# A tuned Fourier-and-MLP kernel: one forward product and a second inverse table for batch 0, angles by integer shifts, filter copies by GpSimd in one row

## The chip, the cores and the metric

One core of one Trainium2 chip. The metric is the time of one execution on the device in microseconds (us), the median of several. "Dense stage" below is the MLP part, which fills most of the time; "prologue" is what batch 0 needs before it.

## The reference, cut to what matters

```python
# x: (8, 3008, 256), filt_r, filt_i: (1505, 256), w_in: (256, 2048), w_out: (2048, 256)
X = np.fft.rfft(x, axis=1)
y = np.fft.irfft(X * (filt_r + 1j * filt_i)[None], n=3008, axis=1)   # per batch
h = y.reshape(-1, 256) @ w_in
out = (0.5 * h * (1 + erf(h / sqrt(2)))) @ w_out                      # (24064, 256)
```

The transform is done as matmuls over 3008 = 47 x 64. For batches 1 to 7 its four stages (s1 to s4, with two trips through HBM, "R") are strewn between the matmuls of the dense stage. Batch 0 has nothing to hide behind: its stages c1, c1t, c2, c3, c3t and c4 stay on the chip and are the prologue.

## The kernel before

Cuts are marked "...".

```python
def load_filters(self, k0, k):          # 4 DMAs from GpSimd into partitions 0..63 of F
    ...
def dup_filters(self, eng, k0, k):      # copies to partitions 64..127, two k at a time
    for k in range(k0, k0 + k, 2):
        o, i = (self.F[r:r + 64, :, k:k + 2, :].rearrange(...) for r in (64, 0))
        eng.tensor_copy(out=o, in_=i)

def c2(self, p):                        # forward product of batch 0, times the filter
    ps = self.bank("ps_c2", "w")        # two banks: plain and turned by a quarter
    for t, o in ((0, 1), (1, 0)):
        for i in range(2):
            nc.tensor.matmul(ps[:, t, ...], lhsT=self.T2[:, k, o:o + 2]..., rhs=...)
    nc.vector.tensor_tensor(out=w, in0=ps, in1=f, op=ALU.mult)          # 128 x 1024

def s1(self, b, c):                     # first stage of batch b >= 1, in slots of the dense stage
    a = self.pa.tile([128, 2, 4, 256], BF16, tag="a", name="a_sb")      # pa has 3 buffers
    ...                                 # matmuls to PSUM, VectorE evicts to a, SyncE writes a to R

# the order on GpSimd's queue
m.load_x(0, 1, 4); ...
for k, n in ((0, 4), (4, 4), (8, 8), (16, 8)):
    m.load_filters(k, n)
m.dup_filters(nc.gpsimd, 4, 4)
m.load_w_in()
m.dup_filters(nc.gpsimd, 8, 8)
...
m.dup_filters(nc.gpsimd, 16, 8)
...                                     # T1p, table_1_tiles
m.load_x(1); m.load_w_out(0); m.load_w_out(8)
```

Batch 1's s1 runs at slots 1, 5, 9 and 13 of the dense stage (a slot is one pair of matmuls into ps_h); the second matmul of the MLP, which reads w_out, starts at slot 16.

## Time and profile before

| | before |
|---|---|
| median | 773.57 us (four runs, 773.46 to 776.69) |
| first dense matmul starts | 40.55 us |
| TensorE busy from there on | without a hole |
| R writes of batch 1, issue to landing | 2.0 to 4.1 us, median 2.6 |

The prediction shows the page and the chain. TensorE in the timeline of the kernel before (start, length, engine, line, operation, names, shape, count; in brackets the idle time ahead and what ended it):

```profile
49.62 1.47 PE L461 MATMUL ps_h<-y_sb,w_in_sb 128*128 128x512 bf16 x6
50.92 0.60 PE L488 MATMUL ps_o<-w_out_sb,g_sb 128*128 128x256 bf16 x4
```

VectorE's timeline of the same kernel:

```profile
46.74 4.87 DVE L247 CAST a_sb<-ps_s 128x512 bf16<-128x512 f32 x8 [0.29 <-PE ps_s L272]
```

The eight evictions into a_sb of the third and fourth s1 stand in one piece: no buffer is missing.

### The profile page before, as it was taken

How to read it: one execution, taken by the hardware profiler on the slowest of the kernel's cores; microseconds unless marked ns; L12 is line 12 of the kernel's file. 1: busy time of each engine (PE TensorE's matmuls, PEld its weight loads, DVE VectorE, ACT ScalarE, POOL GpSimd, SP SyncE). 2: the span in 40 equal slices, each digit the busy share in tenths (PEclk: the TensorE clock that was granted, in tenths of full speed). 3: DMA queues.
4: the chain of work that ended last, by engine and by line, in shares of the span. 5: the costliest groups of instructions: out<-in, count | busy, mean ns of one | idle time of the engine just before them, and what ended most of it. 6: DMA issues, size and time to landing. Idle time of an engine off the chain costs nothing.

```text
span 772.2 us, 15059 instructions
## 1 busy us (share of the span) xinstructions
PE 763.2 (99%) x6066; PEld 528.7 (68%) x6066; DVE 397.3 (51%) x722; ACT 567.4 (73%) x981; POOL 64.9 (8%) x160
## 2 busy tenths in 40 slices
PE   8999999999999999999999999999999999999998
PEld 4847675676776766677777776666776776766666
DVE  7866755464555645457463664637646366411011
ACT  6879955897568975699656996579865798666663
POOL 7801100020000200011000110001100000000000
PEclk9999999999999999999999999999999999999999
DMA  8894745466253661636516464255553422410111
GB/s 138 145 180 124 150 123 129 128 124 151 57 139 107 138 159 41 192 78 122 143 53 181 85 133 123 79 154 95 124 137 81 139 83 69 123 42 28 42 42 55
DMA packets 87398, 85.66 MB, mean 111 GB/s; under 512 B 6752, under 2 KB 77536, under 8 KB 87328
## 3 DMA queue, kind: packets, MB, share of 16 engines
q1 hardware_dynamic: 78816, 68.70, 31.0%
q0 software_dynamic: 8512, 16.00, 14.9%
q8 instruction: 47, 0.77, 0.4%
q14 instruction: 23, 0.19, 0.1%
HBM read 54.00 MB, written 46.66 MB: 130 GB/s over the span
## 4 chain that ended last, share of the span: by engine, by line
PE 94%; DMA 3%; POOL 2%; issue 0%; DVE 0%; POOLq 0%
PE ps_o L488 43%; PE ps_h L461 42%; PE ps_s L345 2%; PE ps_s L320 2%; PE ps_s L295 2%; PE ps_s L272 2%; DMA x_sb<-in_x_dram 2%; POOL F L96 1%; POOL x_sb L82 1%; DMA F<-in_filt_i_dram 1%; POOL F L91 0%; PE ps_e L478 0%; POOL T1s L258 0%; DVE ost L501 0%; POOL T1p L580 0%
## 5 line engine op out<-in xcount | busy, mean ns | idle before, releaser
L464 ACT ACTIVATE g_sb<-ps_h 128x512 bf16<-128x512 f32 x752 | 438.0, 597 | 182.8 <-PE ps_h L461 172.1
L488 PE MATMUL ps_o<-w_out_sb,g_sb 128*128 128x256 bf16 x2992 | 447.5, 273 | 0.0
L461 PE MATMUL ps_h<-y_sb,w_in_sb 128*128 128x512 bf16 (+3 forms) x1600 | 445.8, 366 | 0.7 <-DMA x_sb<-in_x_dram 0.7
L488 PEld LDWEIGHTS <-g_sb 128*128 128x128 bf16 x2992 | 283.9, 98 | 134.3 <-issue 9.9
L461 PEld LDWEIGHTS <-w_in_sb 128*128 128x128 bf16 x1600 | 154.7, 98 | 23.7 <-issue 1.1
L494 DVE COPY ost<-ps_o 128x512 f32<-128x512 f32 x93 | 63.8, 686 | 143.5 <-PE ps_o L488 143.4
L303 DVE TENSOR_TENSOR p<-ps_s,F 128x512 bf16<-128x512 f32 x84 | 58.1, 691 | 105.9 <-ACT p L302 89.5
L249 DVE TENSOR_SCALAR y_sb<-ps_s 128x376 bf16<-128x376 f32 x112 | 60.9, 548 | 80.5 <-PE ps_s L345 80.5
L247 DVE CAST a_sb<-ps_s 128x512 bf16<-128x512 f32 x112 | 69.3, 682 | 27.7 <-PE ps_s L272 27.7
L247 DVE CAST v_sb<-ps_s 128x512 bf16<-128x512 f32 x84 | 57.4, 684 | 2.9 <-PE ps_s L320 2.6
L301 ACT ACTIVATE p<-ps_s 64x512 bf16<-64x512 f32 x84 | 49.9, 594 | 2.1
L302 ACT CAST p<-ps_s 64x512 bf16<-64x512 f32 x84 | 48.5, 577 | 1.0
L345 PEld LDWEIGHTS <-d_sb 96*128 96x128 bf16 x448 | 30.8, 97 | 25.3 <-DMA d_sb<-R 0.2
L101 POOL COPY gate<-p 1x1 bf16<-1x1 bf16 x48 | 8.5, 178 | 470.3 <-DVE p L305 470.3
L305 DVE TENSOR_TENSOR p<-p 128x512 bf16<-128x512 bf16 x84 | 35.7, 425 | 2.9
L345 PE MATMUL ps_s<-T,d_sb 96*128 96x94 bf16 x448 | 36.3, 204 | 0.0
L304 DVE TENSOR_TENSOR p<-p,F 128x512 bf16<-128x512 bf16 x84 | 34.8, 415 | 0.0
L82 POOL DMA_DIRECT2D x_sb<-in_x_dram x64 | 32.7, 512 | 13.0 <-issue 12.5
L320 PE MATMUL ps_s<-p,T 128*128 128x256 bf16 x168 | 32.1, 273 | 0.0
L295 PE MATMUL ps_s<-b_sb,T 128*128 128x256 bf16 x168 | 32.1, 273 | 0.0
L320 PEld LDWEIGHTS <-T 128*128 128x128 bf16 x168 | 16.4, 98 | 20.1 <-DVE p L305 0.5
L295 PEld LDWEIGHTS <-T 128*128 128x128 bf16 x168 | 16.4, 98 | 13.4
(103 smaller groups left out, 189.1 us busy)
## 6 DMA issues: line engine op xcount, KB each, us to landing
out_dram<-ost SPq DMA_DIRECT2D x93, 256.0 KB, 2.3
x_sb<-in_x_dram POOLq DMA_DIRECT2D x64, 188.0 KB, 3.8
R<-a_sb SPq DMA_DIRECT2D x112, 96.0 KB, 2.1
b_sb<-R SPq DMA_DIRECT2D x28, 384.0 KB, 4.3
R<-v_sb SPq DMA_DIRECT2D x42, 256.0 KB, 3.5
d_sb<-R SPq DMA_DIRECT2D x56, 192.0 KB, 4.7
w_in_sb<-in_moe_w_in_dram POOLq DMA_DIRECT2D x2, 512.0 KB, 7.8
w_out_sb<-in_moe_w_out_dram POOLq DMA_DIRECT2D x2, 512.0 KB, 11.3
```

The source lines that it names most:

```text
L247: self.nc.vector.tensor_copy(out=out, in_=in_)
L249: self.nc.vector.tensor_scalar(out=out, in0=in_, scalar1=scale, scalar2=None, op0=ALU.mult)
L295: nc.tensor.matmul(ps[:, 256 * i:256 * i + 256], lhsT=self.T2[:, k, 1:3].rearrange("p a b -> p (a b)"), rhs=self.st[b, "b", k // 6][:, k % ...
L301: nc.scalar.activation(out=p2[0:64], in_=ps[64:128], func=AF.Copy, scale=-1.0)
L302: nc.scalar.copy(out=p2[64:128], in_=ps[0:64])
L303: nc.vector.tensor_tensor(out=p1, in0=ps, in1=f(0), op=ALU.mult)
L320: nc.tensor.matmul(ps[:, 256 * i:256 * i + 256], lhsT=self.T3[:, k].rearrange("p a b -> p (a b)"), rhs=w[:, 256 * i:256 * i + 256], start= ...
L345: nc.tensor.matmul(ps[:, 94 * i:94 * i + 94], lhsT=d[:, (grp % 2) * 4 + i, 128 * half:128 * half + 128], rhs=t4, start=True, stop=True)
L461: nc.tensor.matmul(ps[:, o:o + n], lhsT=self.w_in_sb[:, dc, jc * 128:jc * 128 + 128], rhs=self.ring[:, dc, off:off + n], start=(dc == 0), ...
L464: nc.scalar.activation(out=self.st["g", t][:, jc, :], in_=ps, func=AF.Gelu)
L488: nc.tensor.matmul(ps[:, tile_i % 2, :], lhsT=g[:, jc, tile_i * 128:tile_i * 128 + 128], rhs=self.w_out_sb[:, jc, :], start=(jc == 0), sto ...
L494: nc.vector.tensor_copy(out=ost, in_=ps)
```

## The change

Intent: batch 0 gets one product in c2 instead of two. The quarter turn moves to the inverse side: T3i is T3 with its halves exchanged and signed, so c3 multiplies the second filter part by T3i. The angles of table 2 are made so large (64 turns are added) that a shift of the float's bits left by 15 leaves the fraction of a turn as an integer, in place of a rounding and a subtraction. GpSimd gets small operations, some of which VectorE and ScalarE had, copies all but the first filters in one row, and issues w_in only after it. Gelu's table load moves behind c3. Fillers on TensorE replace part of the work taken away.

```diff
-        self.T2 = c.tile([128, K1, 3, NB], BF16, name="T2")
+        self.T2 = c.tile([128, K1, 2, NB], BF16, name="T2")
@@ table_2_angle @@
-        v.tensor_scalar(out=r, in0=w, scalar1=RND, scalar2=-RND, ...)
-        v.tensor_tensor(out=w, in0=w, in1=r, op=ALU.subtract)
+        ts(out=self.gen[:, 1, k].bitcast(I32), in0=w[:, k].bitcast(I32), scalar1=15, scalar2=None,
+           op0=ALU.logical_shift_left)
@@ c2 @@
-        for t, o in ((0, 1), (1, 0)):
-            for i in range(2): ...            # four matmuls into two banks
+        for i in range(2): ...                # two matmuls into one bank
-            nc.vector.tensor_tensor(out=w, in0=ps, ...)
+            nc.vector.tensor_tensor(out=w, in0=ps.unsqueeze(1).to_broadcast([128, 2, 512]), ...)
@@ c3 @@
+                        t3 = (self.T3i if t else self.T3)[:, 2 * (p + i) + k]
@@ order of the prologue @@
-    m.p = m.iota(g, "p", ...)
-    m.load_x(0, 0, 1, (0,))
+    m.load_x(0, 0, 8)
+    m.p = m.iota(g, "p", ...)
...
+    m.load_filters(0, 4)
+    m.turn_signs(g)                           # 5 small operations on GpSimd
+    m.weights_4(g)                            # 4, before on VectorE
+    nc.gpsimd.tensor_copy(out=m.T1q, ...)     # before on ScalarE
+    nc.gpsimd.memset(m.vt[:, :, 96, :], 0.0)  # before behind the loads
+    for k, n in ((4, 4), (8, 8), (16, 8)):
+        m.load_filters(k, n)
+    m.dup_filters(nc.gpsimd, 4, 20)
...
+    m.table_4(m.T4c, m.T1q, m.wtc, "n", False)   # VectorE evicts, after c3; before ScalarE, earlier
...
+    m.load_w_in()                             # before: after the second filter copy
     m.load_x(1)
```

## The prediction

> **What bounds the kernel now.** I read the page first, then the chain of waits in order of time for the first 80 us, then the timeline of each engine up to 62 us, last the DMA landings in the stretch where the chain turns into DMA.
>
> The page says that TensorE bounds the kernel, at full granted clock:
>
> ```profile
> span 772.2 us, 15059 instructions
> PE 763.2 (99%) x6066; PEld 528.7 (68%) x6066; DVE 397.3 (51%) x722; ACT 567.4 (73%) x981; POOL 64.9 (8%) x160
> ...
> PE 94%; DMA 3%; POOL 2%; issue 0%; DVE 0%; POOLq 0%
> ```
>
> That is no use for this change: its diff touches only the prologue (batch 0 through the Fourier stages). The chain of waits shows what the prologue hangs on, from 5.88 us to the first matmul of the dense stage:
>
> ```profile
> 5.88 7.07 DMA x_sb<-in_x_dram
> ...
> 15.36 5.87 DMA F<-in_filt_i_dram
> ...
> 21.36 1.88 POOL F L96 x2
> ...
> 24.30 4.99 POOL F L96 x5
> ...
> 30.24 2.98 POOL x_sb L82 x6
> 33.22 7.24 DMA x_sb<-in_x_dram
> 40.46 0.09 issue
> 40.55 0.59 PE ps_h L461 x2
> ```
>
> Columns: start, length, what. The reader is to see a row of deliveries: x of batch 0, then the filters, then GpSimd's copies of the filters to the upper 64 partitions. The last link (x of batch 1, landing 40.46) I do not believe: the first matmul of the dense stage reads only the ring and w_in. VectorE's timeline gives another candidate that ends at the same instant, 39.23 + 1.17 = 40.40:
>
> ```profile
> 16.72 4.82 DVE L388 TENSOR_TENSOR p<-ps_c,F 128x1024 bf16<-128x1024 f32 x4
> 22.43 6.88 DVE L388 TENSOR_TENSOR p<-ps_c,F 128x1024 bf16<-128x1024 f32 x6 [0.88 <-POOL F L96]
> 29.61 1.23 DVE L388 TENSOR_TENSOR p<-ps_c,F 128x1024 bf16<-128x1024 f32 x1 [0.30 <-POOL F L96]
> 30.75 1.27 DVE L392 TENSOR_TENSOR p<-ps_c,F 128x512 bf16<-128x512 f32 x2
> ...
> 33.69 5.56 DVE L247 COPY d_sb<-ps_c3t 96x1024 bf16<-96x1024 bf16 x8 [0.75 <-PE ps_c3t L424]
> 39.23 1.17 DVE L249 TENSOR_SCALAR y_sb<-ps_c 128x376 bf16<-128x376 f32 x2
> ```
>
> So the real path is: filters k = 8 to 15 land at 21.23; one GpSimd copy; from 22.43 VectorE multiplies eight steps almost without a hole to 32.02; a fixed tail of 8.4 us (the last of c3, the transposes, the last inverse stage) to 40.4; then TensorE without a hole to the end. VectorE waited 0.88 us before the fifth multiplication, so everything that ended earlier than 22.43 has 0.9 us to spare. Whatever moves 40.55 moves the end one for one; nothing else does, unless TensorE gets a hole later.
>
> **What the Trainium skill says.** "VectorE: DVE Perf Modes", section "Why PSUM operands drop a tier": an fp32 operand in PSUM holds the multiplication at one element a cycle. Its formula for the fp32 two-tensor add, (N+151)/0.96, gives 1224 ns for 1024 elements; the trace has 1217. So reading one bank twice instead of two banks once should not make it shorter. "ScalarE: Activation LUTs", section "What ACT_TABLE_LOAD costs": 1283 ns a load; the trace has 1283 ns. "DMA: Bandwidth & Descriptors", section "Issuing engines are not separate DMA queues": transfers of all queues run on the same 16 engines and interleave. The trace agrees: at 44 to 46 us the software queue has 118% and the hardware queue 20% of the engines' time. "TensorE: Matmul & The Clock Gate", section "What's actually happening": an idle TensorE falls to half clock. The fillers before and after are there for this; in the trace the fillers and matmuls from 7.3 us run at the fast rate (16 small matmuls in 0.84 us against 1.44 for the first 16), and I expect no change.
>
> **The change part by part.**
>
> *One product instead of two in c2.* 48 matmuls of 256 columns become 24. In the timeline four take 0.60 us, about 0.43 without the pipeline's tail, so 24 x 0.108 = 2.6 us leave TensorE. Two to three fillers of 512 columns a step of the loop come in, 0.21 us each: 0.43 + 0.21 = 0.64 us for 0.43 saved. TensorE per two multiplications: 0.43 (c2) + 0.44 (8 transposes) + 0.89 (16 matmuls of 128 columns) + 0.64 = 2.4 us while transposes last, 2.0 after; VectorE needs 2 x 1.15 = 2.3. I followed four steps from 22 us with two banks for c2: each product is ready 0.1 to 0.6 us before VectorE asks. On the path: 0.
>
> *Second inverse table, T3i.* Two of three parts are turned by ScalarE (four evictions of 256 elements, about 0.4 us each), one by VectorE (two small ones). Against that go two extra evictions of the swap (0.5 us each) and one copy of 0.35. ScalarE comes out level, and lies in the slack. On the path: 0.
>
> *Angles by a shift.* For each half 0.56 (rounding) and 0.96 (subtraction) go, a shift of about 0.6 comes: VectorE is free about 1.9 us earlier, ahead of the first evictions. But c1 waits for x (the last of it lands at 12.96), and after c1 there is the 0.9 us of slack. On the path: 0.
>
> *Gelu's table load* moves from 14.51 to the end of c3. There ScalarE idles 2.29 us, against 1.28 + 0.20: hidden. It makes c1t(1) about 1.4 us earlier, within slack.
>
> *Two x loads ahead of all iotas.* In the row before the first issue starts at 1.33 and the second at 2.11, after two iotas. After, I put the first at about 0.9 and the third 0.7 to 0.9 earlier. From 4 us to 28 the DMA engines are full, so the whole row comes earlier by about 0.45: x done 12.5 instead of 12.96, filters k = 8 to 15 at 20.8 instead of 21.23. GpSimd's new small operations (about 11, some 1.7 us) stand in the 2.8 us in which it waited for x landings between filter issues, so they cost nothing.
>
> *Copies in one row.* The w_in issues (20.09 to 21.2) go from between the copies; but GpSimd then waited for the filters anyway (0.15 us), so only the landing counts: copy at 20.85, fifth multiplication at 22.0, then 7 x 1.15 + 1.27 = 9.3, end 31.3 against 32.02. The 0.3 us wait at 29.61 also goes, since its copy had ended at 28.3 and what came late was TensorE's product. Sum: **0.7 us** earlier. The tail stays 8.4 us (4 + 4 banks for 5 + 3 is no bound: VectorE's 8 x 0.69 and ScalarE's 14 x 0.39 fill it). The dense stage would start at 39.85.
>
> *w_in, x of batch 1, w_out later.* This is the debit. Before, w_in was delivered at 23 to 29, before the gap at 28 to 30 us where DMA carries 10 GB/s. After, it is issued behind the last copy, at about 29.7, in front of x and w_out. Landings before, from issue plus time to landing: x of batch 1 at 33.7 (first) to 42.1 (last), w_out 34.2 + 10.4 = 44.6 and 35.1 + 12.1 = 47.2. w_in is 1.05 MB; at the 195 GB/s which the stretch from 36 to 40 us shows, that is 5.4 us. So with an issue 0.5 us earlier: w_in lands at 37.5 (needed 39.85, fine); x parts at 38.6 to 47.0, each needed at 40.4, 42.8, 45.6 and 48.0 (fine, by 1 us or more); w_out at 49.5 and 52.1, plus about 0.8 for the R writes that now run beside it: 50.3 and 52.9. They are needed 10.4 and 12.1 us after the dense stage starts (before: 50.92 - 40.55, and two slots of 0.87 more): 50.2 and 52.0. Estimated hole in TensorE: **0.9 us**, give or take 0.9.
>
> Sum: 773.6 - 0.7 + 0.9 x (it may well not come, I weigh it at half) = **773.4 us**.
>
> **The rivals.** *A, the weights come late.* The stall in full with slower sharing: if the writes to R take half of the engines, w_out's second part lands near 55 and TensorE stands 3 us: 776. For it: 5.4 us more of transfer in a row that was used to 47.2. Against it: in the trace the software queue kept most of the share while R was written (118% to 20%). *B, the prologue is shorter than I think.* If the filters land earlier because x is issued better, up to 1.5 us may come: 772. Against: the DMA engines are at 1.0 to 1.1 busy from 4 us on, so only the start counts. *C, ScalarE becomes the bound of c1 and eats the slack* (sines, swaps, T3 in one row, 7.5 us of work between 6.4 and 14): c2 starts at 17.5 instead of 16.7, and of the 0.7 nothing is left: 774.3. *D, fillers delay c3 or the last transposes:* two fillers stand between the last c3 and the transposes, where TensorE waited 0.52 us anyway; at most 0.3 us.
>
> **Range and chances.** The span from 772 (B) to 776 (A) with the spread of the runs before (773.46 to 776.69) gives 771.6 to 775.8. Two per cent would be 15.5 us; the whole prologue is 40 us and the change has no hold on the other 732. Faster by over 2%: 0.01; within: 0.98; slower: 0.01.
>
> **What would show it.** Right: the first dense matmul near 39.9; filter copies without a break from about 20.9; multiplications of the same 1217 ns with no wait on GpSimd after the fifth; TensorE waits of 0 to 2 us on w_out near 50 us; no other hole up to the end. Wrong: a first dense matmul earlier than 39 (then the delivery of the filters was not the bound), or later than 40.6 (ScalarE or fillers took it), or holes near 43 to 48 for x.

## More of the kernel before

GpSimd's timeline has, for later, the fifth issue of the filters and the first copies:

```profile
10.49 0.50 POOL L91 DMA_DIRECT2D F<-in_filt_r_dram  x1 [0.41 <-DMA x_sb<-in_x_dram]
18.12 2.02 POOL L96 COPY F<-F 64x1024 bf16<-64x1024 bf16 x2
```

And TensorE in the same kernel, by stretch (the second number is its busy time in 5 us; the third from the right is the granted clock, then DMA share and GB/s):

```profile
50.00:55.00 5.00, 5.00 (x36) 3.30 (x34) 1.61 (x3) 3.77 (x7) 0.00 (x0) 1.00 0.72 164
55.00:60.00 5.00, 5.00 (x37) 3.35 (x35) 0.69 (x1) 3.58 (x8) 0.00 (x0) 1.00 0.79 265
```

## The result, and the profile after

| | before | after |
|---|---|---|
| median | 773.57 us | 780.16 us (four runs, 779.58 to 780.67) |
| first dense matmul | 40.55 | 41.49 |
| hole in TensorE near 52 us | none | 3.65 us |
| granted clock, 55 to 60 us | 1.00 | 0.66 |
| span of the profiled run | 772.2 | 778.9 |

The ratio is 1.0075, interval 1.0048 to 1.0102. Ratios here are the mean time of one kernel's fast runs over that of the other's of the same rounds, so not quite the ratio of the medians. Slower by 0.75% counts as "same" by the 2% rule, but it is clear of the noise. The prediction had 773.4 us, 771.6 to 775.8.

TensorE's timeline of the changed kernel:

```profile
41.49 0.59 PE L478 MATMUL ps_h<-y_sb,w_in_sb 128*128 128x512 bf16 x2 [0.73 <-DVE y_sb L269]
...
50.56 1.04 PE L478 MATMUL ps_h<-y_sb,w_in_sb 128*128 128x512 bf16 x4
55.24 0.66 PE L478 MATMUL ps_h<-y_sb,w_in_sb 128*128 128x512 bf16 x2 [3.65 <-DVE a_sb L267]
55.70 1.06 PE L505 MATMUL ps_o<-w_out_sb,g_sb 128*128 128x256 bf16 x4
...
58.26 0.99 PE L478 MATMUL ps_h<-y_sb,w_in_sb 128*128 128x512 bf16 x2
59.08 0.60 PE L505 MATMUL ps_o<-w_out_sb,g_sb 128*128 128x256 bf16 x4
```

Three things are to be read. The dense stage starts 0.94 us later. Then the hole, at the matmul that needs a bank which the fourth s1 fills and VectorE has not evicted. Then the same four matmuls take 1.06 us where they took 0.60; from start to start a pair and its four take 0.85 us each for 0.43, half speed, up to 59.08. The stretches say so:

```profile
50.00:55.00 5.00, 1.59 (x12) 0.51 (x7) 0.67 (x2) 1.58 (x4) 0.00 (x0) 1.00 1.11 233
55.00:60.00 5.00, 4.76 (x21) 2.59 (x21) 1.98 (x4) 1.79 (x3) 0.00 (x0) 0.66 0.52 120
```

"PE 4.76 busy" in the second line is why a busy share misleads: 21 matmuls instead of 37.

What VectorE waited for, from its timeline:

```profile
47.68 2.48 DVE L267 CAST a_sb<-ps_s 128x512 bf16<-128x512 f32 x4 [0.28 <-PE ps_s L292]
54.49 2.48 DVE L267 CAST a_sb<-ps_s 128x512 bf16<-128x512 f32 x4 [4.33 <-DMA R<-a_sb]
```

The fourth s1 needs the first one's buffer (there are three), and that is free only when its writes to R have landed. Batch 1's sixteen writes to R were issued from 44.43 on and took up to 8.6 us (median 5.7, before 2.6). Where they were is in the DMA view of 46 to 48 us, which lists what each queue moved (packets, MB, share of the 16 engines' time):

```profile
q0 software_dynamic: 628, 0.32, 129.5%
issues: line engine op xcount, KB each, median us to landing
R<-a_sb SPq DMA_DIRECT2D x4, 96.0 KB, 7.8
```

Only GpSimd's queue (x and w_out, late because w_in went first) moves anything. SyncE's queue, with eight R writes issued by then, has no line in this view, nor in that of 44 to 46 us. Nor did GpSimd issue the loads in a row, as it had before (x from 30.19, w_out at 34.22 and 35.1): between them it now waited 5.3 us in all for landings of w_in and x. The last two issues:

```profile
39.45 0.93 POOL L116 DMA_DIRECT2D w_out_sb<-in_moe_w_out_dram  x1 [0.62 <-DMA x_sb<-in_x_dram]
41.97 0.89 POOL L116 DMA_DIRECT2D w_out_sb<-in_moe_w_out_dram  x1 [1.59 <-DMA x_sb<-in_x_dram]
```

The later start comes from GpSimd and VectorE. GpSimd's timeline of the changed kernel:

```profile
9.68 0.55 POOL L92 DMA_DIRECT2D F<-in_filt_i_dram  x1 [0.33 <-DMA x_sb<-in_x_dram]
10.26 0.28 POOL L188 TENSOR_SCALAR q<-p 128x1 f32<-128x1 f32 x1
...
12.93 0.14 POOL L575 MEMSET vt_sb<- 128x64 bf16 x1
13.03 1.19 POOL L92 DMA_DIRECT2D F<-in_filt_r_dram  x2
...
19.75 9.88 POOL L97 COPY F<-F 64x1024 bf16<-64x1024 bf16 x10
```

And VectorE's, where it first waits for the row:

```profile
20.82 6.88 DVE L408 TENSOR_TENSOR p<-ps_c,F 128x1024 bf16<-128x1024 f32 x6 [1.35 <-POOL F L97]
```

The eleven small operations stand from 10.26 to 13.03, the filter loads behind them are issued later, and the row of copies starts at 19.75 instead of 18.12. VectorE waits for it already at the third multiplication (1.35 us) and ends the twelfth at 32.58, before at 32.02. The multiplication itself has not changed: 1.15 us a step in a row.

The books can be closed on the trace, by comparing when the same output copy starts in both. The first output copy is 6.42 us late (57.68 and 64.10): 0.94 of start, 3.65 of hole, and 1.83 of rest. By the starts of the matmuls the hole delays 3.81 us (the view counts its 3.65 from the modelled end of the matmul before), so the half-speed stretch is 1.67. From the output copy at 105.79 on all are 6.74 late up to the end; the further 0.32 comes at the first reads of d_sb, which wait for the R writes of the inverse side. 6.74 is the whole difference of the spans (6.7).

### The profile page after: what moved, and what is told of

It is laid out like the page before. It is cut to its first block, busy times and chain, and to the rows that moved or that the text cites.

```text
span 778.9 us, 15058 instructions
## 1 busy us (share of the span) xinstructions
PE 764.8 (98%) x6060; PEld 527.7 (68%) x6060; DVE 397.2 (51%) x725; ACT 568.1 (73%) x979; POOL 66.9 (9%) x168
## 4 chain that ended last, share of the span: by engine, by line
PE 94%; DMA 3%; POOL 2%; DVE 1%; issue 0%; SPq 0%; POOLq 0%; DVEq 0%
PE ps_o L505 42%; PE ps_h L478 41%; PE ps_s L340 2%; PE ps_s L315 2%; PE ps_s L365 2%; PE ps_s L292 2%; DMA R<-a_sb 1%; POOL F L92 1%; DMA x_sb<-in_x_dram 1%; DMA d_sb<-R 1%; PE ps_c L426 1%; PE ps_c3t L441 0%; DVE a_sb L267 0%; PE ps_c L455 0%; PE ps_warm L259 0%
```

## The experiments

Twelve kernels ran, all with correct results. Theory Q (queue): w_in in front of x and w_out pushes the row back, R writes wait behind it, a_sb buffers run out, TensorE idles and its clock drops. Theory G: what was put on GpSimd's queue delays the start. Rivals: the new arithmetic costs by itself (P, N), the weights alone bind, the slow stretch has nothing to do with the hole.

**1. w_in early.**

```diff
-    m.dup_filters(nc.gpsimd, 4, 20)
+    m.dup_filters(nc.gpsimd, 4, 4)
+    m.load_w_in()
+    m.dup_filters(nc.gpsimd, 8, 16)
...
-    m.load_w_in()
     m.load_x(1)
```

> The changed kernel with one thing put back: w_in is issued by GpSimd after the second filter copy, as before, not behind the whole row. Theory Q (order of the loads): w_in in front of x and w_out makes these 5 us later, the R writes of batch 1 queue behind them, the a_sb buffers do not come free and TensorE stands 3.65 us near 52 us, then runs some 4 us at half clock. With w_in early the hole and the half clock go and only the later start of the dense stage (41.5 for 40.55) is left: 774.5 us, 773.9 to 775.3. Rival P (the new tables, copies and order in the first 41 us are to blame, the hole comes from something they shifted): 778 us or more, with the hole still there.

Measured 775.37 us, just above my range (before in the same rounds 773.84; ratio 1.0019). The hole and the slow stretch are gone, clock 1.00 throughout: 4.8 us come from the place of one load. So P falls for the greater part. But the dense stage starts at 42.44, not 41.5: with w_in's two issues among the copies VectorE waits for GpSimd twice (1.21 and 0.72 us). So the row without w_in in it was worth up to 0.95 us, as the change intended (0.30 of it lies ahead of the copies, which start at 20.05 here and at 19.75 there); its price was just larger.

**2. The kernel before with w_in late.**

```diff
-    m.load_w_in()
     m.dup_filters(nc.gpsimd, 8, 8)
...
     m.table_1_tiles(g)
+    m.load_w_in()
     m.load_x(1)
```

> The kernel before with that one part alone: w_in issued behind all the filter copies, just ahead of x of batch 1. Theory Q: the dense stage starts at 40.5 as before (w_in lands near 37.5), then the hole of 3.5 to 4.5 us at the fourth first-stage group of batch 1 and about 2 us of half clock: 779 us, 778 to 780.5. Rival P: 773.6 us as before, or under 1 us more.

Measured 779.99 us, in the expected range, for another reason:

```profile
42.47 0.71 PE L424 MATMUL ps_c3t<-eye,vt_sb 128*128 128x128 bf16 x5 [4.11 <-POOL vt_sb L417]
```

In the kernel before, GpSimd clears a strip of vt after the loads. With w_in in the row, GpSimd's own issues wait for landings, the memset comes 4 us late, and c3t stands. The run says nothing for Q's route; it shows a reason to move that memset too, as the change did.

**3. Again, with the memset early.**

```diff
+    m.vt = m.pg.tile([128, 2, 97, 32], BF16, tag="g", name="vt_sb")
+    nc.gpsimd.memset(m.vt[:, :, 96, :], 0.0)      # ahead of T1p and the loads
```

> As the second run (the kernel before with w_in behind all filter copies), but with GpSimd's small memset of vt ahead of the loads; in the second run it stood behind them and TensorE waited 4.1 us for it, so that run's number was right for another reason. Theory Q (the end of the hole is set by the row of loads and not by when TensorE comes to it): dense stage starts near 40.6 as before, VectorE then waits for the R writes at the fourth group of batch 1 for 5 us or so, TensorE's hole ends near 55 us as in the changed kernel, and the time is 780 us, 779.2 to 781. Rival S (the parts simply add up, 0.9 of the prologue and 5.5 of hole and clock): 779.1 us or less. Rival P (w_in's place does nothing by itself): 774 us.

Measured 778.60 us, ratio 1.0065. The hole is there: 3.29 us before the matmul at 53.47, VectorE waiting 3.98 for R. So the late w_in alone, in the kernel before, makes most of the loss. The number is under my range and fits S (779.1 or less), but S against Q is not decided: w_in was issued at 29.39 here, 1.2 earlier than in the changed kernel, and the hole ended 1.8 earlier. The dense stage started at 39.88, earlier than in the kernel before, of which more in run 10. The four runs go with their mean clock: 777.47 us at 1.000, 778.50 and 778.69 at 0.998, 780.07 at 0.996. The trace is of the first: its granted clock stays at 1.00 behind the hole of 3.29 us. Traces of the others were not kept, and the kernel before, which has no hole, also has runs at 0.997 (774.82 and 774.66 in the rounds of run 1), so what lowered the clock in them is not shown.

**4. Four a_sb buffers in the changed kernel.**

```diff
-        self.pa = pool("pa", 3)
+        self.pa = pool("pa", 4)        # room: the fillers' operand lies in the angles' buffer
```

> The changed kernel with four a_sb buffers instead of three (the fillers' operand moves into the angles' buffer for room). Theory Q with a_sb as the wait that binds: VectorE no longer waits for the R writes; TensorE goes on to slot 18 and there waits for the second half of w_out (landing 55.4, wanted at about 53.6): a hole of 1.5 to 2.5 us in place of 3.65, the clock may hold: 776.5 us, 775.5 to 778. Rival (the weights alone bind, as the prediction had it): no gain, 779.5 to 780.5.

Measured 778.14 us, 2 us under the changed kernel and just above my range. The trace has what Q says: no wait for R, and behind it the next one in line.

```profile
53.12 0.59 PE L478 MATMUL ps_h<-y_sb,w_in_sb 128*128 128x512 bf16 x2
55.50 0.60 PE L505 MATMUL ps_o<-w_out_sb,g_sb 128*128 128x256 bf16 x4 [1.78 <-DMA w_out_sb<-in_moe_w_out_dram]
```

That is the wait which the prediction had named. It exists, but the R writes bind first and hide it. Two runs at clock 1.000 took 777.38 and 777.57, two at 0.998 took 778.72 and 778.87. The trace is of the first, and its clock holds; whether this hole lowered the clock in the slower two is not shown.

**5. Fillers in the hole.**

```diff
+        if s == 15:
+            fill = m.bank("ps_fill", "o")
+            for i in range(16):
+                nc.tensor.matmul(fill, lhsT=m.ones[:, 0:128], rhs=m.ones, start=True, stop=True)
```

> The changed kernel with 16 fillers of 512 columns (3.4 us at full clock) on TensorE ahead of the matmul that stands in the hole. Theory K (idling dropped the clock, and the slow matmuls from 55.2 to 59.1 us cost about 2 us by themselves): the hole's length stays, the clock stays 1.00 in 55 to 60 us, and the time is 778.2 us, 777.7 to 778.8. Rival (the slow stretch comes from something else, DMA traffic or power): 780.2 us or a little more, clock still about 0.66 there.

Measured 779.28 us, above my range. The clock held in the trace, and the matmuls after the hole run at full speed:

```profile
51.50 3.62 PE L683 MATMUL ps_fill<-ones 128*128 128x512 bf16 x16
55.17 0.59 PE L478 MATMUL ps_h<-y_sb,w_in_sb 128*128 128x512 bf16 x2
55.60 0.60 PE L505 MATMUL ps_o<-w_out_sb,g_sb 128*128 128x256 bf16 x4
```

The first output copy starts 1.74 us earlier than in the changed kernel; 0.07 of it is a hole that ends earlier (55.17 for 55.24), and the other 1.67 is the slow stretch. So the slow stretch is what idling did. But only 1.0 of it reaches the end: the output copy that stands at 105.79 in the kernel before is 5.62 late where it was 6.74, since TensorE comes earlier to d_sb reads that are set by the R traffic. My 778.2 left that out.

**6. Small operations off the filter loads.** As run 1, and:

```diff
-    m.load_filters(0, 4)
     m.turn_signs(g)
-    m.weights_4(g); T1q copy; vt memset           # now after the row of copies
+    m.load_filters(0, 4)
```

> The first run (w_in early) and GpSimd's eleven small operations moved out from between the filter loads: the signs of the turn ahead of the first filter load, the weights, T1q and the memset behind the copies. Theory G (these 2.8 us delayed the filter issues by 1.6 us, the copies with them, and so the multiplications): first copy at 18.2 to 18.6 instead of 20.05, dense stage starts at 40.6 to 41.2 instead of 42.44, 774.0 us, 773.6 to 774.6. Rival F (the filters' landing or ScalarE's longer row binds, the small operations hide in the waits for x as the prediction said): dense stage within 0.4 us of 42.4, 775.2 us.

Measured 775.08 us. The copies start at 18.71 (run 1: 20.05), the dense stage at 41.09 (42.44): G holds, F falls. Runs 7, 8 and 11 have the same head, and their copies start at 18.61, 18.42 and 18.22; those of the changed kernel and of runs 4 and 5 at 19.75, 19.67 and 19.56. But the time is above my range: it moved only from 775.37 to 775.08, because the operations moved behind the copies now delay the issue of x of batch 1 to 32.14, and a short wait for R comes back (0.71 us at TensorE).

**7. T4c on ScalarE, one step earlier.**

```diff
-    m.table_4(m.T4c, m.T1q, m.wtc, "n", False)
     ...
+            m.table_4(m.T4c, m.T1q, m.wtc, "n", "act")    # ahead of the last c3
             m.c3(10, 1)
```

> The run before this one, and T4c built one step earlier and evicted by ScalarE, ahead of Gelu's table load. Theory T (TensorE's transposes waited 0.27 us for VectorE's eviction of T4c because they take over its bank): the tail from the end of the multiplications to the dense stage falls from 8.9 to 8.5-8.6 us; 773.7 us, 773.3 to 774.3, 0.2 to 0.4 under the run before. Rival: VectorE or ScalarE sets the tail anyway; no difference.

In the trace the tail from the twelfth multiplication to the dense stage falls from 8.91 to 8.71 us (before: 8.53) and the wait for T4c is gone. In the time (773.7 was expected) it can't be seen: 775.37 us median against 775.08.

**8. VectorE copies k = 8, 9 itself.**

```diff
-    m.dup_filters(nc.gpsimd, 8, 16)
+    m.dup_filters(nc.gpsimd, 10, 14)
...
+        if q == 2:
+            m.dup_filters(nc.vector, 8, 2)
```

> The run before this one, and VectorE makes the copy for k = 8 and 9 itself, in the time in which it waits for GpSimd to make it; GpSimd's row starts at k = 10. Theory F2 (with the filters landing at 21.2 the fifth multiplication hangs on one slow GpSimd copy of 1.04 us; VectorE's takes 0.43): multiplications end 0.4 to 0.6 us earlier, dense stage at 40.1, 773.1 us, 772.6 to 773.7. Rival: the copy costs VectorE what it saves, no difference from the run before.

A plain failure: 782.68 us. The groups of 20 to 30 us, with mean length of one in ns at the end of the middle part:

```profile
L97 POOL COPY F<-F 64x1024 bf16<-64x1024 bf16 x8 | 8.0, 1042 | 0.0
L97 DVE COPY F<-F 64x1024 bf16<-64x1024 bf16 x1 | 6.8, 6799 | 0.0
```

VectorE's copy took 6.8 us, where the same copy takes 0.43 at 16 us with GpSimd not copying. It began at 21.87 and ended at 28.67, 0.3 us after GpSimd's row of seven (21.46 to 28.38). The Trainium skill, "SBUF — State Buffer", section "Terms", says of the port pair that VectorE and GpSimd share that it is locked for the whole instruction and that the loser "fully blocks". The trace agrees and is harsher: VectorE did not get in between two copies of 1.04 us, it sat out the row. The multiplications are not hit: in the changed kernel six of them beside GpSimd's row (20.82 to 27.70) keep 1.15 us a step. They read one operand from PSUM, but no run tests that this is why. Not all of the 7.3 us above run 7 is the copy itself: TensorE stood too, and its granted clock was 0.77 in 30 to 40 us.

**9. GpSimd's queue as light as before.** Run 7, with x's first loads after the first iota as before, the weights back on VectorE and T1q back on ScalarE.

```diff
-        ts = self.nc.gpsimd.tensor_scalar          # weights_4
+        ts = self.nc.vector.tensor_scalar
-    nc.gpsimd.tensor_copy(out=m.T1q, ...)
+    nc.scalar.copy(out=m.T1q, ...)
```

> The changed kernel's arithmetic (second table, shift, one product) with all its new load on GpSimd taken back: w_in early, the turn's signs ahead of the filters, T4c on ScalarE, and now also x's first loads after the first iota as before, the weights on VectorE and T1q on ScalarE. Theory G (the loss sits in what was put on GpSimd's queue, the new arithmetic is neutral): copies start at 18.1 to 18.4, x of batch 1 is issued near 30.3, no wait for R, dense stage at 40.4 to 40.7; 773.9 us, within 0.4 of the kernel before. Rival N (the new arithmetic itself costs, by ScalarE's longer row or the fillers): 774.8 us or more, as in the run without these.

Measured 774.02 us against 773.91, ratio 0.9995 (0.998 to 1.001): the same. No wait on R. The new table, the shift, the single product and the fillers are together worth nothing and cost nothing. Copies and the dense stage started a shade later (18.54 and 40.74) than I expected; N falls.

**10. The kernel before with w_in between copies.**

```diff
     m.dup_filters(nc.gpsimd, 16, 4)
+    m.load_w_in()
+    m.dup_filters(nc.gpsimd, 20, 4)               # and the memset early
```

> Towards a kernel better than both: the kernel before with the memset early and w_in between the filter copies of k = 19 and 20. Theory L (before, w_in's 1.05 MB ran beside the last filters and delayed those for k = 8 to 15 from 20.4 to 21.2; GpSimd's row gains 0.17 us a copy on VectorE, so after six copies w_in's issue of 1.1 us costs nothing): fifth multiplication at 21.5 instead of 22.4, dense stage at 39.8 to 40.1; x of batch 1 comes 1 to 1.5 us later than before and the R wait is 0 to 0.5 us: 773.3 us, 772.9 to 774.0. Rival: the R wait takes all of it, 774.5 or more.

Measured 774.48 us, above my range, ratio 1.0006 (0.9988 to 1.0023): no gain. But the multiplications run as theory L said:

```profile
16.41 12.22 DVE L388 TENSOR_TENSOR p<-ps_c,F 128x1024 bf16<-128x1024 f32 x10
```

Ten multiplications in one piece, where before VectorE stood 0.88 us after the fourth; the dense stage starts at 39.89. L's reason is not shown, though. In run 2, too, w_in came late, and GpSimd still waited 1.04 us, to 21.46, for the filters of k = 8 to 15. And up to the first copies the code of the kernel before and of runs 2, 3 and 10 is the same, yet these start at 18.12, 18.40, 17.80 and 17.81: half a microsecond in the head is no more than traces of one code differ by. What was won goes back at R (0.36 us) and at the first d_sb reads (0.2).

**11. Run 8 with ScalarE's copy.**

```diff
-            m.dup_filters(nc.vector, 8, 2)
+            nc.scalar.copy(out=<F, upper half, k = 8, 9>, in_=<lower half>)
```

> The failed run with the copy for k = 8 and 9, this time made by ScalarE in VectorE's place. In that run the copy took VectorE 6.80 us, as long as GpSimd's whole row, and not 0.43. Theory B (VectorE's fast copy and GpSimd's row shut each other out from SBUF, ScalarE's does not): the copy takes about 1.0 us, the multiplications run on, 775 us. Rival D (the copy or what follows it waits for GpSimd's row by a dependency on F): as slow as that run, 782 us.

```profile
21.40 1.04 ACT L610 COPY F<-F 64x1024 bf16<-64x1024 bf16 x1
```

1.04 us beside the same row of GpSimd, 775.21 us (one run, state unknown). So run 8 was no dependency on F: the block is between VectorE and GpSimd.

**12. All that helped.** Run 9, with w_in as in run 10 and four a_sb buffers as in run 4 (T2 is smaller now, which gives part of the room).

> The eighth kernel (new arithmetic, GpSimd's queue as light as before) with w_in moved between the filter copies of k = 19 and 20 as in the ninth and with four a_sb buffers as in the third. Theory L with Q: no wait of VectorE on filter copies after the third multiplication, dense stage at 39.8 to 40.3, no wait on R, w_out lands before it is wanted: 773.3 us, 772.8 to 773.8, 0.5 under the kernel before. Rival: what is won at 40 us is given back at the first d_sb reads near 100 us, as in the ninth run: 773.9 to 774.5.

(It counts kernels by label: its third, eighth and ninth are runs 4, 9 and 10 here.)

Measured 773.29 us (773.01 to 773.74) against 773.88, ratio 0.9992 (0.9979 to 1.0006). Dense stage at 39.47, no wait on R, every output copy from 105.79 on 0.92 us ahead of the profiled run of before. It is the fastest median of all kernels here, by less than its interval can separate from the kernel before.

| run | dense stage starts | TensorE waits 45 to 57 us | median, before in the same rounds |
|---|---|---|---|
| changed kernel | 41.49 | 3.65, R | 780.16, 773.57 |
| 1 w_in early | 42.44 | none | 775.37, 773.84 |
| 3 before, w_in late | 39.88 | 3.29, R | 778.60, 774.01 |
| 4 four buffers | 41.41 | 1.78, w_out | 778.14, 773.84 |
| 6 small operations moved | 41.09 | 0.71, R | 775.08, 774.01 |
| 9 GpSimd as before | 40.74 | none | 774.02, 773.91 |
| 10 before, w_in between | 39.89 | 0.36, R | 774.48, 773.91 |
| 12 all | 39.47 | none | 773.29, 773.88 |

## Why the prediction was wrong

Its frame held: the change acts through the start of the dense stage and through holes after it, and the page's shares say nothing of either. Its sum did not. One of its own signs of being wrong came, a first dense matmul later than 40.6 (41.49), but not from ScalarE or the fillers, which it named: runs 6 and 9 put it on GpSimd's queue. By its own steps:

- **"GpSimd's new small operations ... cost nothing" failed.** They were put at 1.7 us inside 2.8 us of waiting. They took 2.77 us, gaps included, and the wait in which they were to hide stood in front of later issues, not of one place: the issue after them came at 13.03 instead of 10.49. Run 6 moved them and the dense stage came 1.35 us earlier.
- **"The whole row comes earlier by about 0.45" failed.** The last x landed at 13.3 us (issued at 5.9, 7.4 to landing), not at 12.5. The third load starts at 2.81 instead of 3.38, but the fifth to eighth are issued when they were, and the DMA moved 153 GB/s in 5 to 10 us where it had moved 182. Why the rate was lower stays open.
- **Of the 0.7 us gained in the sum, 0.94 were lost instead.** 0.56 of it lies before the end of the multiplications, 0.38 in the tail, which I had kept at 8.4: T4c's eviction made the transposes wait, and run 7 got 0.20 back. The last 0.18 were not tested. The trace has VectorE stand 0.22 us for TensorE before its last eviction, in runs 1, 6, 7, 9, 11 and 12 as well and not in the kernel before; the prediction had put the 4 + 4 banks there as no bound, which no run tests. (31.3 + 8.4 is 39.7, not the 39.85 that the prediction took from 40.55 - 0.7.)
- **The debit failed most.** It was 0.9 us at half weight, on w_out. It was 3.65 us, and the wait was for a_sb buffers. The lateness of w_out was rightly computed in kind: its second half was put at 52.9 and landed at 55.4 (GpSimd's waits between its issues were left out), and with R out of the way TensorE waits 1.78 us for it (run 4). But the R writes were counted only as traffic that slows w_out (0.8 us). That they would be held up themselves, and the a_sb buffers with them, was left out. Rival A carried the evidence and I read it the wrong way round: "the software queue kept most of the share while R was written (118% to 20%)" was put against the rival. It says that the R writes get little, and R writes hold buffers.
- **A term was missing.** This hole in TensorE cost its length and then the clock: 1.67 us, by the books and by run 5, half of the 3.4 us in which the matmuls ran at half speed (55.70 to 59.08). Not every hole does: in the traces the clock holds behind 1.78 (run 4) and 3.29 us (run 3), and falls with 3.65 here and with 4.11 in run 2 (0.57 in 40 to 45 us). I had cited "TensorE: Matmul & The Clock Gate" for the fillers, that an idle TensorE falls to half clock, and not applied it to my own hole.
- **What held:** the multiplication's length, the products off the path, ScalarE and Gelu's load hidden, the shift neutral (together: run 9), and w_in landing in time for itself.

## What to carry to other kernels

When a load is moved, ask not only when it is wanted, but which other queue's small transfers will stand behind it and which buffers those hold. Time a hole on TensorE as its length plus the slow stretch that may follow it; here it followed holes of 3.65 and 4.11 us and not those of 1.78 and 3.29. And an engine that only issues and copies, as GpSimd here, is a queue in order: a microsecond of small work put "into its waits" shifts everything behind it.

## What the Trainium skill lacked or had wrong

- "DMA: Bandwidth & Descriptors", section "Queues, rings and completion order": each engine is said to take the queues in turn, packet by packet. Here the hardware queue, with R writes issued from 44.43 on, moved nothing up to 48 us while the software queue used 119% and 130% of the engines' time; its landings went from a median of 2.6 to 5.7 us. The page has no figure for such a wait, and the runs do not show its mechanism.
- "SBUF — State Buffer", section "Terms", the shared port pair: it says that the loser waits until the other's instruction is over. In run 8 VectorE's copy of 0.43 us waited through seven GpSimd copies in a row, 6.80 us. ScalarE's copy beside them took 1.04 us.
- No page that I looked up gives a time for GpSimd's tiny operations: eleven of them, nine on 128 x 1, took 0.14 to 0.34 us each, and 2.77 us in a row with the gaps between them.
